# Turnings of the first weight in other PSUM banks, two copies ahead of roundings, and two banks for the last sum, in a fused attention and maxout feed-forward kernel

## The chip, the cores and the metric

The kernel runs on one core of one Trainium2 chip. Its time is the device time of that core in microseconds (us), given as the median of several runs. One execution was also taken with the hardware profiler. All times of instructions below come from that one execution; its span runs from the first to the last instruction that the profiler saw, and its own device time is a little longer than the span.

The engines: TensorE (PE, matrix products; its loads of the stationary operand are listed apart as PEld), VectorE (DVE), ScalarE (ACT), GpSimd (POOL), and SyncE (SP), which here only issues transfers. Each works through its own instructions in program order. PSUM is the memory into which PE writes its products, eight banks of 128 x 512 words of 32 bits; all other data is in SBUF.

## The reference, cut to what matters

```python
# attention: B, H, S, D = 4, 8, 768, 48
f = 1 / (1 + exp(-f_logit))
for t in range(S):
    state = f[:, :, t, :, None] * state + k[:, :, t, :, None] * v[:, :, t, None, :]
    y[:, :, t] = einsum('bhd,bhde->bhe', q[:, :, t], state)
# bridge: heads side by side, x is 3072 x 384
x = y.transpose(0, 2, 1, 3).reshape(3072, 384)
# feed-forward: w1, w2, w3 are 384 x 768, w_out is 768 x 384
h = maximum(maximum(x @ w1, x @ w2), x @ w3)
out = h @ w_out
```

## The kernel before, in words

**Attention.** The sequence is cut into chunks of 64 tokens. A unit is one chunk of two batches with all heads, so 128 rows; there are 24 units, numbered u. For each unit the gates are sigmoids (L308), a scan over them gives the decay from each token to the chunk's end (`scan`, L329), another scan gives the decay from the chunk's start (`before`, L347). k and q are brought to features on partitions by PE transposes (`transposed`, L291), for the early units that matter here, and multiplied with these decays. `keys` transposes the weighted keys (copy ks), `pairs` multiplies keys and queries of a chunk (L392) and masks the result on DVE (L395), `values` multiplies that with v (L407/L411), `sums` makes the chunk's contribution to the state (L436), which for the first two units is copied into the state by ACT (L442) and later added on DVE. `y_by_tokens` copies a finished unit of the first group out of PSUM on ACT, and `x_of_tokens` transposes it on PE and copies it on ACT into `xT`, the transposed x that the feed-forward reads.

**Feed-forward.** Four units make a group of 512 tokens; there are six groups. Groups 1 to 5 use `ffn`, in which products of pairs of blocks are saved by sums taken beforehand (`inputs_by_pairs`, matmuls at L819, and `outputs_by_pairs`, L611, whose helpers `into`, `read` and `add` issue the matmuls, the ACT copies L616 and the DVE additions L619). Group 0 uses `ffn_first`, since the weights are still arriving: `product` (L537) multiplies x with w2 - w1 and w3 - w1, six blocks j of 128 columns, the first three blocks in two half groups of 256 tokens and the last three with all 512. ACT copies the first of each pair to `hm` (L748), DVE takes the maximum with the second and with zero (L750). What is missing, x times w1 w_out, is a linear term: each block of w1 is transposed on PE and written back by ACT (`turn`, L721), and at the end `linear` (L728) multiplies the turned w1 with w_out.

**Weights.** They come as 24 pieces of 384 KB: 18 of w1, w2 and w3, in turn for each block j, and six of w_out. They lie in DRAM as 64-bit numbers, and each piece is rounded to 32 bits: `round_begin` issues two or three ACT activations (L240, L241, L244), `round_end` one or two DVE operations (L251 to L254) and one POOL addition (L258). `round_to(n)` issues `round_end` of the pieces up to n and the `round_begin` of one piece more. `apart` (L699) then subtracts the w1 block from w2 on POOL and from w3 on DVE. `ffn_first` calls `round_to(ROUNDED[n_step])` and `load_weights` after each of its 18 steps, and turns block `TURNED[n_step]` after six of them.

**Order.** The order on each engine is written out by hand: the program is issued as the code stands. `fill(ns)` stands between the attention's steps and draws as many steps of the feed-forward's generator as have that length by an estimate of the matmuls' time. So all that is issued between two steps of `ffn_first` (turning, rounding, transfers) stands in each engine's queue between the attention's instructions around it.

**Banks.** The PSUM pools hand out banks in turn: two named `tr` (attention's transposes of f, k, q, keys and x), one named `a` (pairs, and the first units' sums), one named `y` (values), and two named `p` (the feed-forward). A tile that draws a bank waits until the last reader of the tile that had it has finished. `bank(in_tr)` draws a feed-forward bank from `tr` instead of `p`.

```python
def bank(in_tr=False):
    if in_tr:
        return ps_tr.tile([128, TOK], FP32, name="tr")
    return ps_f.tile([128, TOK], FP32, name="p")
```

q of the first three units is transposed into a `p` bank, that of later units into a `tr` bank, and so is k.

**The start.** Around the change the prologue runs `values(1)`, `y_by_tokens(1)`, `keys(2)`, `round_to(2)`, `sums(1)`, `x_of_tokens(1)`, `scan(3)`, `pairs(2)`, `after(3)` (k), `carry(3)`, `round_to(3)`, `before(3)` (q), `values(2)`, and then the first steps of `ffn_first`.

**The end.** For the last group `outputs_by_pairs` stores its four tiles of 128 tokens as soon as they are ready: each is two transfers of 96 KB (`store`, L556). The second transfer of the last two units is issued on ACT's queue, the others on SP's. The last tiles are made by `into(c, 0, s4, ...)`, an addition of one half on DVE, a store, `into(c, 1, s4, ...)`, the addition of the other half, a store. Both halves lie in one bank, c.

After the last store a flag is read that says whether inputs or weights were outside the range that this fast path takes (L1296); it isn't set here, and the second path is not run.

Of the kernel before, what the change touches and what calls it, by code (L numbers as in the profile page):

```python
# [9 lines left out]
FP32 = mybir.dt.float32  # L10
# [45 lines left out]
def kernel(  # L56
# [12 lines left out]
    nc = tc.nc  # L69
    B, H, S, D = q.shape  # L70
    HP = H // 2
    NU = B // 2 * (S // C)
    UT = 2 * C
    DM = H * D
# [3 lines left out]
    GRP = 4  # L78
    TOK = GRP * UT
# [10 lines left out]
    def fast():  # L90
        ctx = ExitStack()
        with ctx:
# [4 lines left out]
            ps_f = ctx.enter_context(tc.tile_pool(name="ps_f", bufs=2, space=bass.MemoryType.PSUM))  # L97
# [263 lines left out]
            def keys(u):  # L361

                if u < min(BY_ROWS, NU - 2):
                    kh = ready[u]["kh"]
                    tr_s = ps_tr.tile([UT, HP, 128], FP32, name="tr")
                    for hp in range(HP):
                        nc.tensor.transpose(tr_s[:, hp, :], kh[:, hp].rearrange("p a t -> p (a t)"), ident)
                    ks = work.tile([UT, H, DP], FP32, name="ks")
                    nc.scalar.copy(ks.rearrange("s h d -> s (h d)"), tr_s.rearrange("s a d -> s (a d)"))
                    ready[u]["ks"] = ks  # L370
# [114 lines left out]
            def x_of_tokens(u, xT):  # L485
                x = ready.pop(u)["x"]
                tr_x = ps_tr.tile([128, NK, UT], FP32, name="tr")
                for kt in range(NK):
                    nc.tensor.transpose(tr_x[:, kt, :], x[:, kt * 128:(kt + 1) * 128], ident)
                nc.scalar.copy(by_halves(xT)[:, u // 2, :, u % 2 * UT:(u % 2 + 1) * UT], tr_x)  # L490
# [36 lines left out]
# [4 lines that stand above are left out]
# [20 lines left out]
            def store(u, o):  # L551
                c, bp = divmod(u, 2)
                for a in range(2):
                    t0 = (2 * bp + a) * S + c * C
                    last = u >= NU - 2 and a
                    (nc.scalar if last else nc.sync).dma_start(out=out[t0:t0 + C, :], in_=o[a * C:(a + 1) * C, :])  # L556

            def outputs(hm, xT, i):
# [40 lines left out]
            def outputs_by_pairs(g, hm, xT):  # L599
# [9 lines left out]
                def into(b, p, lhs, rhs):  # L609
                    for k in range(HJ):  # L610
                        nc.tensor.matmul(b[:, p * HD:(p + 1) * HD], lhsT=lhs(p)[:, k], rhs=rhs[:, k],  # L611
                                         start=id(b) not in begun, stop=(k == HJ - 1), skip_group_check=True)
                        begun.add(id(b))
# [4 lines left out]
                def add(out, b, n, at=slice(0, 2)):  # L618
                    nc.vector.tensor_tensor(out[:, at], pairs_of(b[:, 0:DM])[:, at], pairs_of(partial[n])[:, at], op=ALU.add)  # L619
# [19 lines left out]
                into(a, 1, s2, w_mix[1])  # L639
                read(a, 1)  # L640
                yield COST
                into(c, 0, s1, w_mix[0])
                yield COST
                into(c, 1, s1, w_mix[0])
                nc.scalar.copy(tops[:, 2], c[:, 0:DM])
                yield COST
                into(a, 0, A(0, 1), w_mix[2])
                yield COST
# [7 lines left out]
                yield COST  # L656
                into(c, 0, X(0), lin[1])
                yield COST
                into(c, 1, X(0), lin[1])
                yield COST  # L660
                into(a, 0, A(1, 1), w_mix[3])
                yield COST
# [14 lines left out]
                    add(o_of(0, 1), c, 1, slice(0, 1))  # L677
                    store(g * GRP, o_four[:, 0])
                yield COST
                into(c, 1, s4, corner(1, 1))  # L680
                if last:
                    add(o_of(0, 1), c, 1, slice(1, 2))
                    store(g * GRP + 2, o_four[:, 2])
                else:
                    add(o_of(0, 1), c, 1)
                    late.extend((g * GRP + i, o_four[:, i]) for i in (1, 3, 0, 2))
# [16 lines left out]
            def round_to(count):  # L703

                for n in range(rounded[0], min(count, len(pieces))):
                    if n + 1 < len(pieces):
                        round_begin(n + 1)
                    round_end(n)
                    if n < 3 * NJ and n % 3 == 1:
                        apart(n, nc.gpsimd)  # L710
                    if n <= 3 * NJ and n and n % 3 == 0:
                        apart(n - 1, nc.vector)
                    rounded[0] = n + 1

            def turn(j):

                p = ps_f.tile([128, TOK], FP32, name="p")
                piece = w_in[0][:, :, j * 128:(j + 1) * 128]
                for a in range(NK):
                    nc.tensor.transpose(p[:, a * 128:(a + 1) * 128], piece[:, a, :], ident)  # L720
                nc.scalar.copy(piece, p[:, 0:DM].rearrange("q (a c) -> q a c", a=NK))  # L721
                yield DM * COLUMN
# [9 lines left out]
                            nc.scalar.copy(w_nat[:, a, :], p[:, 0:DM])  # L732
                        yield 2 * DM * COLUMN

            ROUNDED = (5, 7, 8, 10, 10, 11, 11, 12, 12, 13, 14, 15, 16, 17, 18, 20, 21, 22)
            TURNED = {3: 0, 4: 1, 6: 2, 14: 3, 16: 4, 18: 5}

            def ffn_first(xT):
# [188 lines left out]
            with tc.manual_schedule():  # L927
# [39 lines left out]
                values(1)  # L967
                y_by_tokens(1)
                keys(2)
                round_to(2)  # L970
                sums(1)
                x_of_tokens(1, xT)
                scan(3)
                pairs(2)
                after(3)
# [354 lines left out]
```

## Time and profile before

| | |
|---|---|
| runs (us) | 426.46, 426.51, 427.65 |
| median | 426.51 us |
| the profiled execution | 427.35 us |
| its span | 425.5 us |
| PE busy | 405.3 us (95%), 4650 instructions |
| loads on PE (PEld) | 340.3 us (80%) |
| DVE busy | 265.4 us (62%) |
| POOL busy | 232.8 us (55%) |
| ACT busy | 179.9 us (42%) |
| transfers | 47.20 MB, mean 111 GB/s |
| chain that ended last | PE 86%, DVE 3%, SP's queue 3%, ACT 2%, transfers 2% |

How to read what is quoted later. The page draws the span as 40 slices of 10.6 us; a digit is the busy share of an engine in tenths, and 9 means 90% or more. `PEclk` is the clock granted to PE in tenths of full speed. In the view of waits a line names who waits (engine, tile, line), whom it waited for after `<-` (engine, tile, line), then the total in us, how many waits, and the longest. In the timeline a line gives start and duration in us, engine, line, operation, what it writes and reads with the shapes, how many instructions it puts together, and in brackets the idle time of the engine before it with what ended it. A wait for several semaphores is put down to the one that came last by the profile. In a view of windows the columns are the stretch, its length, the busy time of PE with the instruction count, the mean granted clock, the busy share of the transfer engines, and GB/s.

### The profile page before, as it was taken

To read this page: it belongs to the slowest core of one execution; us is meant where nothing else is said; L and a number is where in the kernel's file an instruction comes from. 1 tells how busy PE (TensorE), PEld (TensorE's weight loads), DVE (VectorE), ACT (ScalarE), POOL (GpSimd) and SP (SyncE) were. 2 spreads that over 40 slices of the span, in tenths; PEclk is the share of its full clock that TensorE was granted. 3 is DMA by queue.
4 is the path that set the end of the run, shared out by engine and by line. 5 is a ranking of instruction groups with operands and counts; after the bars stand their busy time and mean duration, and the time that the engine had idled before them with its cause. 6 is when DMAs were issued, how large, how long until landed. Compare 5 with 4: busy or idle time off the path is not lost.

```text
span 425.5 us, 11548 instructions
## 1 busy us (share of the span) xinstructions
PE 405.3 (95%) x4650; PEld 340.3 (80%) x4650; DVE 265.4 (62%) x517; ACT 179.9 (42%) x413; POOL 232.8 (55%) x260
## 2 busy tenths in 40 slices
PE   5988799899999999999999999999999999999993
PEld 4766665466567888998889988889988899988993
DVE  6986574952687699868789867888774720012300
ACT  2459566732114442425531444442264424576210
POOL 2178354541888676386586357566546960425600
PEclk9989999999999999999999999999999999999998
DMA  8988987771547753276645276634473011542003
GB/s 170 227 262 259 262 241 119 123 173 51 93 95 119 90 128 54 64 96 103 109 122 109 41 116 81 142 82 87 70 151 86 0 53 42 141 129 66 2 1 78
DMA packets 174617, 47.20 MB, mean 111 GB/s; under 512 B 154016, under 2 KB 172256, under 8 KB 174560
## 3 DMA queue, kind: packets, MB, share of 16 engines
q1 hardware_dynamic: 171216, 45.61, 51.6%
q10 hardware_dynamic: 3344, 0.81, 0.9%
q8 instruction: 37, 0.61, 0.6%
q14 instruction: 20, 0.16, 0.1%
HBM read 37.75 MB, written 4.72 MB: 100 GB/s over the span
## 4 chain that ended last, share of the span: by engine, by line
PE 86%; DVE 3%; SPq 3%; ACT 2%; DMA 2%; issue 1%; POOL 1%; DVEq 0%; POOLq 0%
PE p L819 19%; PE tr L819 16%; PE p L611 14%; PE tr L611 12%; PE p L564 6%; PE p L537 5%; PE p L728 3%; PE y L500 3%; PE y L411 3%; PE a L392 2%; DMA raw<-in_moe_w_dram 2%; SPq L174 2%; PE y L436 2%; PE tr L291 1%; SPq L164 1%
## 5 line engine op out<-in xcount | busy, mean ns | idle before, releaser
L819 PE MATMUL tr<-xT,placed 128*128 128x256 f32 x300 | 73.3, 385 | 0.0
L382 DVE STREAM_TRANSPOSE ks<-kh 32x128 f32<-32x128 f32 x224 | 67.7, 302 | 4.6 <-POOL kh L340 1.0
L819 PEld LDWEIGHTS tr<-xT,placed 128*128 128x128 f32 x300 | 55.6, 190 | 9.1 <-ACT hm L827 1.4
L819 PE MATMUL p<-xT,placed 128*128 128x256 f32 x180 | 45.0, 381 | 0.0
L819 PEld LDWEIGHTS p<-xT,placed 128*128 128x128 f32 x180 | 33.8, 190 | 4.7
L537 PE MATMUL p<-xT,w_in 128*128 128x256 f32 (+1 forms) x108 | 34.3, 458 | 2.9 <-DVE hm L750 2.2
L619 DVE TENSOR_TENSOR o<-tr,w_in 128x384 f32<-128x384 f32 (+1 forms) x11 | 5.7, 514 | 49.6 <-PE tr L611 44.3
L329 DVE TENSOR_TENSOR_SCAN r<-gate,from_one 128x520 f32<-128x520 f32 x24 | 31.3, 1306 | 8.3 <-ACT gate L308 5.3
L340 POOL TENSOR_TENSOR kh<-kt,r 128x512 f32<-128x512 f32 x16 | 28.8, 1798 | 10.6 <-DVE kt L296 10.6
L837 POOL TENSOR_TENSOR hm<-hm,rest_bits 128x512 f32<-128x512 f32 x15 | 22.7, 1512 | 19.1 <-ACT hm L827 19.1
L597 POOL TENSOR_TENSOR w_in<-hm 128x256 f32<-128x256 f32 x15 | 10.9, 727 | 40.5 <-DVE hm L870 40.5
L347 DVE TENSOR_TENSOR_SCAN prod<-gate,from_inv 128x520 f32<-128x520 f32 x24 | 32.5, 1355 | 0.0
L506 ACT COPY xT<-y 64x256 f32<-64x256 f32 (+1 forms) x60 | 22.1, 369 | 24.1 <-PE y L500 23.4
L395 DVE TENSOR_TENSOR at<-a,mask 128x512 f32<-128x512 f32 x24 | 16.5, 688 | 24.2 <-PE a L392 23.9
L258 POOL TENSOR_TENSOR w_in<-top_bits,rest_bits 128x384 uint32<-128x384 uint32 x18 | 21.8, 1211 | 15.5 <-DVE top_bits L254 8.8
L819 PE MATMUL p<-w_in,placed 128*128 128x256 f32 x120 | 30.0, 379 | 0.0
L862 DVE TENSOR_TENSOR hm<-tr,hm 128x512 f32<-128x512 f32 x15 | 10.2, 681 | 29.3 <-PE tr L819 19.3
L537 PEld LDWEIGHTS p<-xT,w_in 128*128 128x128 f32 x108 | 19.3, 190 | 10.7 <-issue 6.2
L655 POOL TENSOR_TENSOR o<-top_bits,w_in 128x384 f32<-128x384 f32 x5 | 5.1, 1015 | 41.6 <-ACT w_in L616 41.6
L616 ACT COPY w_in<-p 128x384 f32<-128x384 f32 x15 | 7.2, 479 | 47.1 <-PE p L611 47.1
L280 ACT ACTIVATE raw<-top_bits 128x384 f32<-128x384 f32 x48 | 25.2, 526 | 0.4
L819 PEld LDWEIGHTS p<-w_in,placed 128*128 128x128 f32 x120 | 22.8, 190 | 3.1
(153 smaller groups left out, 890.5 us busy)
## 6 DMA issues: line engine op xcount, KB each, us to landing
raw<-in_moe_w_dram SPq DMA_DIRECT2D x24, 384.0 KB, 4.2
v_ld<-in_v_dram SPq DMA_DIRECT2D x48, 96.0 KB, 3.2
placed<-in_moe_w_dram SPq DMA_DIRECT2D x12, 384.0 KB, 6.6
out_dram<-o SPq DMA_DIRECT2D x46, 96.0 KB, 2.4
placed<-in_moe_w_out_dram SPq DMA_DIRECT2D x6, 384.0 KB, 6.0
raw<-in_moe_w_out_dram SPq DMA_DIRECT2D x6, 384.0 KB, 3.4
f_ld<-in_f_logit_dram SPq DMA_DIRECT2D x32, 64.0 KB, 2.6
k_ld<-in_k_dram SPq DMA_DIRECT2D x32, 64.0 KB, 2.5
```

The source lines that it names most:

```text
L258: nc.gpsimd.tensor_tensor(dst, by(top), by(rest), op=ALU.add)
L280: nc.scalar.activation(over, size, AF.Relu, scale=(-1 / HI_MIN, 1.0)[step - 1], bias=(1.0, -HI_END * (1 - 2.0 ** -24))[step - 1], accum_ou ...
L329: nc.vector.tensor_tensor_scan(r[:, 0:LEN][:, ::-1], flat(gate)[:, ::-1], flat(from_one)[:, ::-1], 1.0, op0=ALU.mult, op1=ALU.max)
L340: (nc.vector if u < BY_ROWS else nc.gpsimd).tensor_tensor(kh.rearrange("p h a t -> p a h t"), kt, by_batch(r[:, 1:LEN + 1].rearrange("p (x ...
L347: nc.vector.tensor_tensor_scan(flat(prod), flat(gate_tiles[u % 2]), flat(from_inv[u % 2]), 1.0, op0=ALU.mult, op1=ALU.max)
L382: nc.vector.transpose(ks[n * 32:(n + 1) * 32, :, par, e0:e0 + 32], kh[p0:p0 + 32, :, a, t0:t0 + 32])
L506: nc.scalar.copy(xT[o, :, t0 + a * C:t0 + (a + 1) * C], y[i, a, 0:HP * C].rearrange("p (h t) -> p h t", h=HP))
L537: nc.tensor.matmul(p if w < TOK else p.rearrange("p (two t) -> p two t", two=2), lhsT=w_in[i][:, kt, j * 128:(j + 1) * 128], rhs=x[:, t.st ...
L564: nc.tensor.matmul(p[:, 0:DM], lhsT=lhsT, rhs=rhs, start=(n == 0), stop=(n == NJ + NK - 1))
L611: nc.tensor.matmul(b[:, p * HD:(p + 1) * HD], lhsT=lhs(p)[:, k], rhs=rhs[:, k], start=id(b) not in begun, stop=(k == HJ - 1), skip_group_c ...
L819: nc.tensor.matmul(b[:, j * HALF:(j + 1) * HALF], lhsT=w[:, (2 * n + j) * 128:(2 * n + j + 1) * 128], rhs=x, start=begin and j == 0, stop= ...
L837: nc.gpsimd.tensor_tensor(out(n, 0), out(n, 0), first, op=ALU.add)
```

## The change

It has four edits.

1. In the prologue, `sums(1)` and `x_of_tokens(1)` move ahead of the rounding of the next weight pieces: `round_to(2)`, `sums(1)`, `x_of_tokens(1)` becomes `sums(1)`, `round_to(1)`, `x_of_tokens(1)`, `round_to(2)`. On ACT the state copy (L442) then stands ahead of two roundings, and the x copy ahead of one.
2. `turn` draws its bank from `tr` for the blocks j = 3, 4 and 5 (`J_HALF` is 3), and from step 13 to the end `ROUNDED` is one piece higher.
3. In `store`, the second transfer of all four units of the last group goes to ACT's queue: four transfers on each queue instead of six and two.
4. In `outputs_by_pairs`, for the last group, the second half of the last sum goes to another bank, b, which is free by then; the copy of the bank's first contents (`tops`) is split into two ACT copies of half the width, one from each bank, and the last addition reads d.

```diff
             def store(u, o):
-                    last = u >= NU - 2 and a
+                    last = u >= NU - GRP and a
...
             def outputs_by_pairs(g, hm, xT):
+                d = b if last else c
                 into(c, 0, s1, w_mix[0])
                 yield COST
-                into(c, 1, s1, w_mix[0])
-                nc.scalar.copy(tops[:, 2], c[:, 0:DM])
+                if last:
+                    begun.discard(id(d))
+                    nc.scalar.copy(pairs_of(tops[:, 2])[:, 0], c[:, 0:HD])
+                into(d, 1, s1, w_mix[0])
+                if last:
+                    nc.scalar.copy(pairs_of(tops[:, 2])[:, 1], d[:, HD:DM])
+                else:
+                    nc.scalar.copy(tops[:, 2], c[:, 0:DM])
...
-                into(c, 1, X(0), lin[1])
+                into(d, 1, X(0), lin[1])
...
-                into(c, 1, s4, corner(1, 1))
+                into(d, 1, s4, corner(1, 1))
                 if last:
-                    add(o_of(0, 1), c, 1, slice(1, 2))
+                    add(o_of(0, 1), d, 1, slice(1, 2))
...
             def turn(j):
-                p = ps_f.tile([128, TOK], FP32, name="p")
+                p = bank(j >= J_HALF)
...
-            ROUNDED = (5, 7, 8, 10, 10, 11, 11, 12, 12, 13, 14, 15, 16, 17, 18, 20, 21, 22)
+            ROUNDED = (5, 7, 8, 10, 10, 11, 11, 12, 12, 13, 14, 15, 16, 18, 19, 21, 22, 23)
             TURNED = {3: 0, 4: 1, 6: 2, 14: 3, 16: 4, 18: 5}
...
                 keys(2)
+                sums(1)
+                round_to(1)
+                x_of_tokens(1, xT)
                 round_to(2)
-                sums(1)
-                x_of_tokens(1, xT)
                 scan(3)
```

## The prediction

> **What bounds the kernel.** The page first: TensorE (PE) is busy 95% of the span and holds 86% of the chain that ended last, so what counts is where PE waits. I read PE's waits next, from 20 to 100 us and from 130 us to the end; then the timeline around each wait; then windows cut where the granted clock steps; then the queues at the end.
>
> ```profile
> PE   5988799899999999999999999999999999999993
> PEclk9989999999999999999999999999999999999998
> ```
> ```profile
> PE p L537 <- DVE hm L750: 2.2, 3, 0.9
> PE a L392 <- ACT st L442: 1.8, 1, 1.8
> ...
> PE p L728 <- POOL state L357: 0.6, 1, 0.6
> ```
> ```profile
> PE tr L611 <- DVE o L619: 0.5, 1, 0.5
> ```
>
> Each line gives total, times and longest. The four parts of the change aim at these four lines: 1.80 us at 21.67, three waits of 0.68, 0.61 and 0.92 at 48.80, 67.17 and 76.77, 0.61 at 84.38, and 0.52 at 418.20. After 130 us PE waits for nothing else: what is won or lost before 100 us reaches the end unchanged.
>
> The first wait, in the timeline (start, duration, engine, line, operation):
>
> ```profile
> 22.50 0.56 ACT L244 ACTIVATE rest_bits<-raw 128x384 uint32<-128x384 uint32 x1 [0.38 <-DMA raw<-in_moe_w_dram]
> ...
> 22.97 0.45 ACT L442 COPY st<-a 128x384 f32<-128x384 f32 x1
> ...
> 23.47 0.75 PE L392 MATMUL a<-qh,kh 48*64 48x64 f32 x32 [1.80 <-ACT st L442]
> 24.16 1.11 PE L291 MATMUL tr<-ident,k_ld 128*128 128x128 f32 x4
> ```
> And PE windows of 3.41 us (length, PE busy, granted clock, DMA share, GB/s):
> ```profile
> 20.54:23.95 3.41, 1.61 (x68) 1.00 0.44 101
> 23.95:27.36 3.41, 3.41 (x48) 0.50 0.99 302
> ...
> 41.02:44.43 3.41, 2.07 (x40) 1.00 1.08 376
> ```
> A window with 1.61 us of PE work (47%) is followed by one at half clock; one with 2.07 us (61%) is not. So a wait costs its length and, where it empties a window, a slow window as well.
>
> **Part 1, state and x copies ahead.** ScalarE's (ACT's) state copy now follows the ks copy (20.96, ends 21.54); its matmuls L436 end at 21.19. It starts near 21.57 instead of 22.97, and the pairs L392 at 22.07, 1.40 earlier. The x copy stands behind one rounding, ends near 22.9, and then lets the q transposes go. What is late next: the values L407 need the masked product L395 on VectorE (DVE), 24.35 to 25.0, behind the scan L329 of 22.96, which stands behind roundings of landed weights and does not move. So L407 starts at 25.05, not 26.05: -1.0. At full clock it takes 1.17 (row of 18.83), not 1.75: -0.6. The first product L537 of the feed-forward follows at 26.2, not 27.73 (GpSimd's difference L699 it needs is done at 26.08): -1.5. The second product at 30.45 gains only 0.35: GpSimd (POOL) works without a gap from 23.19, its sum L258 ends at 29.46 and DVE's L699 follows. But the hm copy on ACT (29.33) moves 1.5, ACT is gapless behind it, and the o copy of 35.93 on the chain moves with it. Then landing limits: weight piece 9 is issued at 34.09 and lands 3.7 later, 37.8, and its rounding ran at 38.77 (-1.0); piece 10, 34.8 plus 4.4, 39.2 against 40.24 (-1.0). Chain alone: -1.9. I take **-1.4**, between. The other end is 0: in an execution whose clock is not halved at 23.95, q would end at 25.05 in the old order too and L407 would start no later than now.
>
> **Part 2, turnings in the transpose banks, roundings one step earlier.** The waits of 67.17 and 76.77 come from the product drawing the bank of the last product, because the turning has taken the other one; these go (-0.61, -0.92). The wait at 84.38 is put down to POOL's state, but the instruction waits for DVE and POOL, and DVE's hm, 83.54 to 84.23, frees its bank: it goes as well (-0.61). The one at 48.80 stays, since turning 2 keeps its bank. A new wait comes. There are two transpose banks; after the turning of j = 4, k draws one and q draws the turning's own. So q must wait for ACT's copy of the turning, last in this queue:
>
> ```profile
> 73.96 0.60 ACT L308 ACTIVATE gate<-tr 128x512 f32<-128x512 f32 x1
> 74.45 0.55 ACT L240 ACTIVATE top_bits<-placed 128x384 f32<-128x384 f32 x1
> ...
> 76.90 0.55 ACT L244 ACTIVATE rest_bits<-placed 128x384 uint32<-128x384 uint32 x1
> 77.35 0.46 ACT L721 COPY w_in<-p 128x384 f32<-128x384 f32 x1
> ```
>
> Gate, six rounding activations, copy: done at 77.81, or 77.2 with the 0.61 won before. Moving the roundings does not shorten it: two of them still stand ahead of this copy. PE ends k near 74.65 and stands 2.5 us. Behind q in PE's order wait product, values and sums, and none can pass. The product starts at 77.65 instead of 76.77: +0.88; with -0.61 at 84.38, **+0.25** in all. Ends: -2.1 (no new wait) and +0.9 (the wait at 84.38 stays).
>
> The rounding moved up costs nothing while its covers hold: three activations (1.5 us) fall before ACT's idle 67.05 to 70.02, DVE's two operations (0.55 each) into its 5.02 us idle before 73.27. Without those covers they would delay the masked product by up to 1.1. The w1 copy of turning 3, 0.8 later, is wanted only by the f transposes at 72.5.
>
> Clock: 2.5 us of standing in windows of 3.41. Halving needs between 1.34 us (39% idle, not enough) and 1.80 us of idle in one window. Over all positions of the window that happens in (3.41 + 2.5 - 2T)/3.41, 68% (T = 1.80) to 95% (T = 1.34). Price: dense PE work at half clock for at most 3.41 us, 1.7; part of the slow window may fall into the standing itself. I take **+1.3**, ends 0 and 1.7.
>
> The Trainium skill, page "TensorE: Matmul & The Clock Gate", section "HAM oscillation — how this bites in real kernels", lets the clock fall only after gaps of more than about 3.4 us. This trace differs: it fell after 1.80 us. By the page the 2.5 us would not halve the clock and the sum would be 424.7; the measurement decides.
>
> **Parts 3 and 4, the end.**
>
> ```profile
> 417.29 4.66 SPq L556 DMA_DIRECT2D out_dram<-o  x6
> ...
> 418.20 1.24 PE L611 MATMUL tr<-w_out,w_in 128*128 128x192 f32 x6 [0.52 <-DVE o L619]
> 419.48 0.36 DVE L619 TENSOR_TENSOR o<-tr,w_in 128x192 f32<-128x192 f32 x1 [1.33 <-PE tr L611]
> ```
>
> With its own bank the second half follows the first: 416.70 + 0.97 = 417.67 instead of 418.20, and the pipe is not refilled; DVE's last addition moves from 419.48 to about 418.75 and ends at 419.1: -0.74. The one copy L645 (0.48) becomes two of half the width; ACT stands idle 3.42 us before its next copy at 410.89, which hides them, and PE asks for neither bank before 410.7. SP now issues its six stores between 417.29 and 420.4, where the last starts 0.56 after its data is ready and takes 1.51 to issue; the last completion SP waits for comes at 423.7. With four per queue the last two go at 419.13. They land 2.4 (the first stores' landing) to 3.3 us (the last one's) later, 421.5 to 422.4; eight stores of 96 KB at the 215 to 240 GB/s of that stretch need 3.3 to 3.7 us from 418.2, so 421.5 at the least. Gain 1.3 to 2.2; if the transfers fill the time whatever the queues, 0.74. I take **-1.5**. From 423.7 to 425.5 nothing changes.
>
> The skill's page "DMA: Bandwidth & Descriptors", section "Issuing engines are not separate DMA queues", says that a second issuing engine saves only issue time, usually small. By that the split would add 0.56 to the 0.74, and the sum would be 0.2 higher.
>
> **The sum.** The profiled execution took 427.35 (span 425.5 and 1.85 around it): 427.35 - 1.4 + 0.25 + 1.3 - 1.5 = **426.0**. It stands 0.84 above the median of 426.51 (runs 426.46, 426.51, 427.65); I read the difference as mostly the slow window at 23.95, which not every execution needs to have.
>
> **Rivals.**
> - Forecast, the standing at q happens and halves the clock: 426.0. For it: bank order and ACT's queue are fixed by the program, and 47% was enough to halve. Chance 0.50.
> - The standing happens, the clock stays: 424.7. For it: 61% was not enough to halve, and the window's position is free. Against: 2.5 us is longer than the 1.80 that did it. 0.28.
> - The slow window only moves, from 24 us to 77 us. Most executions then have no early gain (start at the lower runs, 426.5), pay 0.25 and the full 1.7, and get only the 0.74 at the end: 427.7, slower than before. It decides as soon as the window around q has under about half PE work and the one around 22 us had more. For it: the runs shown spread over 1.2 us, the size of such a window. Against: ACT's o copy is on the chain. 0.15.
> - The stores do not do what they should, because the last landing is set by the transfers: 426.0 + 0.76 = 426.8. 0.07.
>
> **The numbers.** About 0.3% (1.28 us: 425.23 to 427.79) is what a measurement of this kernel can tell from no change. Faster: most of the second case (0.24) and a fifth of the first (0.10), 0.34. Slower: about half of the third, 0.08. The rest, 0.58, is within. The range runs from below the second case (its early gain at 1.9) to the third less 0.3: 424.0 to 427.4.
>
> **What would show it.** L392 starts near 22.1 and its wait is under 0.5; no slow window at 24; L407 at 25. Waits of L537 for hm at 67 and 77 gone; instead the q transposes wait some 2.5 us for ACT's w_in copy, followed by about 3.4 us at clock 0.5. The L611 wait for DVE o is gone; both queues issue their last store within 0.1 us after DVE's last addition, and the last completion comes 1.3 to 2.2 us earlier. I would be wrong if q does not wait, if half clock spreads over a second window, or if product L537 at 27.7 has not moved.

## The result, and the profile after

Over 20 runs each, the changed kernel takes **427.65 us** against **427.37 us**: ratio 1.0002, 95% interval 0.9988 to 1.0016. That is no change that can be measured. The forecast was 426.0 with a range up to 427.4, so the time lies just outside it, on the side of the third rival. The kernel before has come out higher as well: three runs had given 426.51. One of the changed kernel's 20 runs took 595.28 us at a granted clock of 0.66; such slow runs are left out of every ratio here.

The profiled execution of the changed kernel has a span of 426.5 us against 425.5, +1.0 where the sum on record has -1.35. The same instruction in both timelines shows where it came from (start, us; the last two rows are ends):

| instruction | before | after | difference |
|---|---|---|---|
| pairs L392 of unit 2 | 23.47 | 21.89 | -1.58 |
| values L407 of unit 2 | 26.05 | 24.96 | -1.09 |
| first product L537 | 27.73 | 26.05 | -1.68 |
| second product | 30.45 | 30.35 | -0.10 |
| fourth product | 37.15 | 36.78 | -0.37 |
| check of the state L473 | 43.33 | 43.47 | +0.14 |
| product near 48.8 | 48.80 | 48.95 | +0.15 |
| q transposes L291 | 75.25 | 77.15 | +1.90 |
| state product L500, next unit | 87.56 | 89.19 | +1.63 |
| last sum, first half L611 | 416.54 | 418.18 | +1.64 |
| last addition L619 | 419.84 | 420.69 | +0.85 |
| span | 425.5 | 426.5 | +1.0 |

The page shows the one slow window, now in the eighth slice, 75 to 85 us (before, a digit 8 in the third):

```profile
PEclk9999999899999999999999999999999999999999
```

So part 1 ends at +0.15 (on record -1.4), part 2 with the clock costs 1.49 (on record 1.55), and parts 3 and 4 give 0.65 (on record 1.5). These are differences between two single executions; that of before had a half clock at 24 us, that of the changed kernel has none there.

PE's waits in the changed kernel, from 15 to 135 us (who <- whom: us in total, times, longest):

```profile
PE tr L291 <- ACT w_in L728: 2.4, 1, 2.4
PE p L537 <- DVE w_in L706: 2.2, 2, 1.7
PE p L473 <- DVE st L444: 1.5, 1, 1.5
PE y L407 <- DVE at L395: 1.3, 1, 1.3
```

The wait for ACT's state copy is down to 0.3. In its place PE waits for DVE, on three lines (L473's wait was 1.0 before), and at q for ACT's w_in copy, 2.4 us as foreseen. In the early timeline (start, duration, engine, line, operation, idle time before and what ended it):

```profile
21.89 0.69 PE L392 MATMUL a<-qh,kh 48*64 48x64 f32 x32 [0.26 <-ACT st L442]
24.96 1.17 PE L407 MATMUL y<-v_ld,at 64*64 64x48 f32 x32 [1.35 <-DVE at L395]
...
30.35 1.56 PE L537 MATMUL p<-xT,w_in 128*128 128x256 f32 x6 [1.68 <-DVE w_in L706]
```

Of the 1.6 us won at L392 and at the first product all but 0.10 is given back in the 1.68 before the second. Around q, the row of its transposes and windows of 3.41 us laid on the steps of the clock (stretch, length, PE busy, granted clock, share of the transfer engines, GB/s):

```profile
77.15 1.04 PE L291 MATMUL tr<-ident,q_ld 128*128 128x128 f32 x4 [2.44 <-ACT w_in L728]
```
```profile
73.90:77.31 3.41, 0.97 (x9) 0.99 0.79 102
77.31:80.73 3.42, 3.42 (x8) 0.51 0.59 69
```

The standing (PE without work until q can start) leaves PE 0.97 us of work in a window, and the next window is at half clock. And the end (the queues' lines give first issue and total stretch):

```profile
418.92 3.01 SPq L556 DMA_DIRECT2D out_dram<-o  x4
418.93 3.30 ACTq L556 DMA_DIRECT2D out_dram<-o  x4
...
420.33 0.36 DVE L619 TENSOR_TENSOR o<-tr,w_in 128x192 f32<-128x192 f32 x1 [0.55 <-PE tr L611]
```

The two halves follow each other without the 0.52 us wait, but the last stores go out at 421.39 (SP) and 421.61 (ACT), 0.7 and 0.9 after the last addition.

### The profile page after: what moved, and what is told of

The parts are those of the page before. It is cut to its first block, busy times and chain, and to the rows that moved or that the text cites. A ratio compares the mean times of both kernels' runs of the same rounds, so it can differ in the third digit from the quotient of the medians.

```text
span 426.5 us, 11551 instructions
## 1 busy us (share of the span) xinstructions
PE 404.1 (95%) x4650; PEld 339.3 (80%) x4650; DVE 266.2 (62%) x517; ACT 179.9 (42%) x414; POOL 233.1 (55%) x260
## 4 chain that ended last, share of the span: by engine, by line
PE 87%; SPq 5%; DMA 2%; ACT 2%; POOL 1%; DVE 1%; issue 1%; ACTq 0%
PE p L826 19%; PE tr L826 16%; PE p L611 14%; PE tr L611 11%; PE p L537 6%; PE p L564 6%; PE y L411 3%; PE y L500 3%; PE p L735 3%; SPq L164 2%; PE a L392 2%; PE y L436 2%; SPq L174 2%; DMA placed<-in_moe_w_dram 2%; PE tr L291 1%; SPq L218 1%
## 5 line engine op out<-in xcount | busy, mean ns | idle before, releaser
L537 PE MATMUL p<-xT,w_in 128*128 128x256 f32 (+1 forms) x108 | 35.6, 471 | 3.5 <-DVE w_in L706 2.2
L619 DVE TENSOR_TENSOR o<-tr,w_in 128x384 f32<-128x384 f32 (+1 forms) x11 | 5.7, 515 | 48.8 <-PE tr L611 43.5
L506 ACT COPY xT<-y 64x256 f32<-64x256 f32 (+1 forms) x60 | 22.1, 368 | 24.1 <-PE y L500 23.4
L258 POOL TENSOR_TENSOR w_in<-top_bits,rest_bits 128x384 uint32<-128x384 uint32 x18 | 21.8, 1217 | 15.4 <-DVE top_bits L254 7.7
L537 PEld LDWEIGHTS p<-xT,w_in 128*128 128x128 f32 x108 | 19.9, 196 | 11.9 <-issue 5.6
L280 ACT ACTIVATE raw<-top_bits 128x384 f32<-128x384 f32 x48 | 25.2, 526 | 0.4
```

The lines of the kernel that those rows point to most:

```text
L258: nc.gpsimd.tensor_tensor(dst, by(top), by(rest), op=ALU.add)
L280: nc.scalar.activation(over, size, AF.Relu, scale=(-1 / HI_MIN, 1.0)[step - 1], bias=(1.0, -HI_END * (1 - 2.0 ** -24))[step - 1], accum_ou ...
L506: nc.scalar.copy(xT[o, :, t0 + a * C:t0 + (a + 1) * C], y[i, a, 0:HP * C].rearrange("p (h t) -> p h t", h=HP))
L537: nc.tensor.matmul(p if w < TOK else p.rearrange("p (two t) -> p two t", two=2), lhsT=w_in[i][:, kt, j * 128:(j + 1) * 128], rhs=x[:, t.st ...
```

## The experiments

The experiments set the theory on record (ACT's copies are what PE waits for early; the standing at q halves the clock; four stores a queue land earlier) against a rival for each part that the traces suggested. Every kernel was compared with the kernel before on the same chip; the medians of before were 427.79, 427.42, 427.33 and 427.65 in the four groups.

| kernel | us | ratio to before (95%) | half clock in its profile, us |
|---|---|---|---|
| p1_only | 427.43 | 0.9991 (0.9977 to 1.0005) | 30.4 |
| p2_only | 428.24 | 1.0012 (0.9997 to 1.0027) | 76.7 |
| end_only | 427.0 | 0.9982 (0.9965 to 0.9999) | none |
| after_turn4_in_p | 424.92 | 0.9931 (0.9910 to 0.9952) | 24.9, 45.4 |
| light_weights | 425.4 | 0.9965 (0.9941 to 0.9989) | none |
| light_weights_p1 | 424.54 | 0.9934 (0.9916 to 0.9953) | 44.4 |
| after_filler | 427.21 | 0.9997 (0.9983 to 1.0010) | 30.2, 43.9 |
| turn4_in_p_early | 429.11 | 1.0043 (1.0024 to 1.0063) | 25.6 |
| after_filler_5 | 426.28 | 0.9980 (0.9966 to 0.9993) | none |
| turn4_in_a | 423.07 | 0.9898 (0.9876 to 0.9919) | 30.6 |
| stores_only | 426.84 | 0.9989 (0.9975 to 1.0004) | none |
| turn4_in_p_old_roundings | 425.63 | 0.9957 (0.9939 to 0.9974) | none |
| light_dve | 425.43 | 0.9948 (0.9933 to 0.9963) | none |
| light_pool | 424.23 | 0.9929 (0.9912 to 0.9947) | 23.4 |
| turn4_in_a_no_part1 | 423.85 | 0.9923 (0.9909 to 0.9936) | none |
| turn4_in_a_old_stores | 423.93 | 0.9923 (0.9906 to 0.9940) | 45.4 |

The last column gives where each half-clock stretch of the profiled execution begins. Each is one window of 3.41 us, except that of turn4_in_p_early, which is two. Those after the last matmul are left out.

**Each part alone.** p1_only is part 1 in the kernel before:

```diff
                 keys(2)
-                round_to(2)
                 sums(1)
+                round_to(1)
                 x_of_tokens(1, xT)
+                round_to(2)
```

> Part 1 alone in the kernel before. The theory on record: -1.4 us, whichever execution, because the copies were the last thing PE waited for. New theory (the stream of weights is the bound from 24 to 50 us: both profiles issue pieces 9 to 11 at 34.1 to 34.2 and the first use after that moved only from 40.73 to 40.44, then to +0.15): between -0.4 and +0.2 us. In its profile L392 starts near 22 and L407 near 25 by both; by the new theory the check matmul L473 near 43.3 and the product near 48.8 stay within 0.3 us of the kernel before, counted from the first weight's landing.

-0.4 us (-1.0 to +0.2). L392 starts at 21.78 and L407 at 24.59, but the product near 48.8 is at 48.84: nothing is left of it there. The new theory's number holds, at its edge; its cause, the landings of the weights, does not (below). The profiles with a full clock up to 50 us say the same: this product starts at 48.24 to 49.17 in the old order (p2_only, end_only, stores_only, turn4_in_a_no_part1) and at 48.23 to 48.95 in the new (the changed kernel, after_filler_5, turn4_in_p_old_roundings).

p2_only has the new banks for the turnings and the new `ROUNDED`:

> Part 2 alone (turnings of j = 3, 4, 5 in the transpose banks, later roundings one earlier) in the kernel before. Theory: PE stands 2.4 us at the q transposes near 77 for ACT's w_in copy, the clock is halved for 3.41 us after it, +0.25 for the waits and +1.7 for the clock where it is halved: +1.0 to +2.0 us. Rival (the standing only takes the place of other waits and the clock has no part): 0 to +0.3 us, with no window at clock 0.5 after 77 us.

+0.5 us (-0.1 to +1.2) in time, so under what was expected of it; in the profile the 2.4 us wait at L291 and the half clock at 76.7 are there. From the product that starts at 57.47 before (56.91 here) to the third group of L500 it is 46.78 us, the same as in the changed kernel and 1.49 more than before (45.29). This stretch hardly varies: in all eight profiles with the old part 2 it is 45.29 or 45.30. That the time shows less than 1.49 would fit executions in which the standing falls across two windows and halves nothing, but no run here shows how many do.

end_only has parts 3 and 4:

> Parts 3 and 4 alone (two banks for the last sum, four stores on each queue). The theory on record: -1.5 us, 0.74 from the bank and the rest from stores that land earlier. New theory, from the profile of the changed kernel: the bank gives 0.7 to 0.8 and the stores nothing, since with two queues issuing at once each issue takes about twice as long (1.1 to 1.2 us against 0.59) and the last store still goes out 0.7 to 0.9 us after the last addition: -0.6 to -0.8 us.

-0.8 us (-1.5 to 0.0). From the copy of the last group's first finished tiles (L677) to the end of the span it is 8.16 us, against 8.80 before (L670) and 8.14 in the changed kernel; how much this varies is told below.

**Where part 2 pays, and the clock.** after_turn4_in_p is the changed kernel with one turning back:

```diff
-                p = bank(j >= J_HALF)
+                p = bank(j in (3, 5))
```

> The changed kernel, with turning j = 4 alone put back into the feed-forward's own banks (3 and 5 stay in the transpose banks). Theory of the standing at q: the 2.4 us wait of L291 goes, the wait of the product L537 for hm near 77 (0.9) comes back, the halved clock after 77 goes; against the kernel before the waits at 67 and 84 stay won (0.6 each) and the end 0.64: -1.5 to -2.0 us against before, and -1.5 to -2.5 against the changed kernel. Rival (weight roundings set the pace there, so that what is won at q is lost at the next weight): within 0.5 us of the changed kernel.

424.92, -2.9 us against before (-3.8 to -2.1): more than forecast, although its profile has two windows at half clock. The product of 57.47 is 0.80 late there (the half clock at 45.4), and the third group of L500 is 0.90 early, so part 2 in this form is worth 1.70: the two waits of 0.61 and some 0.2 us of refilling at each. One bank decides over part 2's sign.

after_filler keeps PE busy during the standing; after_filler_5 does so with the right number of matmuls:

```diff
                         after(n)
+                        if n == GRP + 2:
+                            spare = ps_a.tile([UT, 2, 512], FP32, name="a")
+                            for _ in range(8):
+                                nc.tensor.matmul(spare[:, 0, 0:256], lhsT=ident, rhs=flat(from_one)[:, 0:256], start=True, stop=True)
                         before(n)
```

> The changed kernel, with eight matmuls of 128x256 whose result nobody reads, in the bank of the pairs, put between the k and q transposes where PE stands for 2.4 us near 75. Theory of the clock: the standing keeps its length or grows by at most 0.2 us, but no window near 77 is at half clock any more, so that -1.3 to -1.7 us against the changed kernel; about 426.0. Rival (the half clock does not come from the standing, or comes anyway): the same time as the changed kernel within 0.3 us.

> The changed kernel with five unread matmuls between the k and q transposes near 75, where the run with eight filled 3.62 us and so held q up by about 1 us; five are 2.26 us by that row, a little less than the 2.44 us that PE stands. Theory of the clock: q starts where it does in the changed kernel, within 0.2 us, at full clock, and from the start of one L500 (near 71.4) to that of the next (near 89.2) it is 16.1 us in the profile, 17.8 in the changed kernel; the time is 1.2 to 1.7 us below the changed kernel's, about 426.2. Rival: 17.8 us as before, same time.

The first missed its number: eight such matmuls ran as sixteen passes in 3.62 us and held q up until 78.20, and two early windows were at half clock; the one near 77 was gone there too. The second is the clean test. Its q transposes and the window there:

```profile
76.49 0.66 PE L291 MATMUL tr<-ident,q_ld 128*128 128x128 f32 x4 [0.34 <-ACT w_in L728]
```
```profile
73.45:76.86 3.41, 3.07 (x18) 1.00 0.78 96
76.86:80.28 3.42, 3.42 (x51) 1.00 0.63 89
```

The standing is as long, but it is filled; the clock stays, the stretch from the first group of L500 to the second takes 16.21 us against 17.82 in the changed kernel, and the time is -0.9 us against before (-1.5 to -0.3), where the changed kernel has +0.1; by the ratios that is 0.9 won, a little under what was expected. The half clock comes from PE's lack of work in the standing and costs 1.6 to 1.7 us (1.61 here, with q 0.07 later than in the changed kernel, counted from the first group of L500).

turn4_in_a puts turning 4 where no one waits for its copy:

```diff
-                p = bank(j >= J_HALF)
+                p = ps_a.tile([128, 2, 512], FP32, name="a")[:, 0] if j == 4 else bank(j in (3, 5))
```

> The changed kernel with turning j = 4 in the bank of the pairs, which has been free since the masked product of 74.1 and is wanted again at 87; 3 and 5 stay in the transpose banks. Theory of the banks: neither the q transposes nor the product near 76.7 wait, so that the 0.92 us wait and some 0.2 us of refilling go as well: 0.9 to 1.2 us below the run with turning 4 in its old bank, 423.5 to 424.0 us. Rival (what PE waits for there is the weights' rounding, whatever the bank): the same as that run within 0.3 us.

423.07 us, **-4.4 us against before (-5.3 to -3.5), the fastest version here** and a little under the 423.5 that was the least expected. Its timeline at the place of the standing:

```profile
73.92 0.60 PE L291 MATMUL tr<-ident,q_ld 128*128 128x128 f32 x4
74.35 2.74 PE L537 MATMUL p<-xT,w_in 128*128 128x512 f32 x6
```

Neither waits. By the profiles 2.85 of the 4.4 us is part 2 in this form (42.44 from the product of 57.47 to the third group of L500, against 45.29). From the first group of L500 to the second it is 13.48 us, 1.16 less than with turning 4 in its old bank (14.64): the bank, not the rounding, was what PE waited for.

turn4_in_p_old_roundings takes the other half of part 2 out (and has `j in (3, 5)`):

```diff
-            ROUNDED = (5, 7, 8, 10, 10, 11, 11, 12, 12, 13, 14, 15, 16, 18, 19, 21, 22, 23)
+            ROUNDED = (5, 7, 8, 10, 10, 11, 11, 12, 12, 13, 14, 15, 16, 17, 18, 20, 21, 22)
```

> The changed kernel with turning j = 4 back in its old bank and the roundings as they were before. Theory on record: the rounding moved up costs nothing and gains nothing, so that the time is within 0.3 us of the run with turning 4 in its old bank (424.92). Rival (the earlier rounding is what took the wait at 84 away): 0.5 to 0.8 us more, with PE's wait of L735 for POOL back.

425.63, 0.7 more in the medians and 1.1 by the ratios (the two ran on different chips), and the same stretch is 15.29 against 14.64, 0.65 more. The rival is right: with the bank free, the first `linear` waits for the last rounded pieces.

```profile
85.35 0.91 PE L735 MATMUL p<-w_out,w_in 128*128 128x384 f32 x2 [0.38 <-POOL w_out L258]
```

**Where part 1 went.** light_weights leaves the early subtractions out:

```diff
-                    if n < 3 * NJ and n % 3 == 1:
+                    if 9 <= n < 3 * NJ and n % 3 == 1:
                         apart(n, nc.gpsimd)
-                    if n <= 3 * NJ and n and n % 3 == 0:
+                    if 9 < n <= 3 * NJ and n % 3 == 0:
                         apart(n - 1, nc.vector)
```

> The kernel before without the subtraction of w1 from the first six of the w2 and w3 blocks (three of 1.0 to 1.25 us on POOL and three of 0.55 to 1.34 us on DVE, between 25 and 43 us); the output is not the reference's. Theory now: DVE and POOL, with the roundings and these subtractions, end level with the copies of part 1, so taking work from them alone moves the product near 48.8 by 0.5 to 1.5 us. The theory on record (the copies on ACT are what PE waits for): that product stays within 0.3 us.

The product near 48.8 comes at 46.57, 2.2 us earlier, more than either theory had, with ACT's order untouched (L392 at 23.33) and the ninth weight piece landing when it did before (37.57 and 37.77). So neither ACT's copies alone nor the landings were what this product waited for.

> The same with part 1; the same subtractions are left out. Theory now: with DVE and POOL out of the way part 1 is worth something, 0.5 to 1.4 us against the run without part 1, in the product near 48.8 and in the time. Rival (the landings of the weights are the bound, near 29.6 and 38.8 us): below 0.3 us.

The fourth product comes at 35.14 against 35.48, so part 1 is worth 0.34 there; then ACT waits for the ninth weight piece, which landed at 38.15 against 37.57, and the state check comes at 41.66 against 41.09. The rival holds at that place: with DVE and POOL lighter, the landing is next. In time part 1 gives 0.9 us here in the medians, which intervals of 0.8 and 1.0 to either side do not tell from nothing. In both runs the check comes 3.5 us after that landing. In the changed kernel the piece landed at 38.84 and the check came 4.6 us after it, so there the landing was not what held it; but by the same 3.5 us it would have let the check come no earlier than 42.4, 1.0 before the 43.33 of the kernel before. (The product near 48.8, at 48.21, also carries a half clock from 44.4.)

light_dve and light_pool make only the second or only the first of the two edits.

> The kernel before without DVE's three subtractions of w1 from early w3 blocks (0.55, 0.54 and 1.34 us, before 43 us); the output is not the reference's. If DVE holds the stretch: the product near 48.8 comes 1.3 to 2.2 us earlier, as without the subtractions of both engines. If POOL holds it: under 0.5 us.

> The kernel before without POOL's three subtractions of w1 from early w2 blocks (1.0 to 1.2 us each, before 40 us); the output is not the reference's. If POOL holds the stretch: the product near 48.8 comes 1.3 to 2.2 us earlier. If DVE holds it: under 0.5 us.

```profile
46.19 1.56 PE L537 MATMUL p<-xT,w_in 128*128 128x256 f32 x6 [0.68 <-DVE hm L750]
```
```profile
47.49 1.56 PE L537 MATMUL p<-xT,w_in 128*128 128x256 f32 x6 [0.68 <-DVE hm L750]
```

The product near 48.8 in light_dve (first) and light_pool (second): 2.6 and 1.3 us earlier. (light_pool's profile has a half clock at 23.4, light_dve's none.) Neither "under 0.5" came true: both engines are on the chain, in turn. The times say the same (-2.2 and -3.0 us, each interval 0.7 wide to either side), and cannot rank them.

turn4_in_p_early tried the landings:

```diff
                 load_weights(3)
+                load_weights(6)
                 load_v(2)
                 load_v(3)
-                load_weights(6)
```

> The changed kernel with turning j = 4 back in its old bank, as in the run that took 424.92 us, and weight pieces 3 to 8 issued ahead of the v tiles of units 2 and 3, so that they land about 1 us earlier. Landing theory: the product near 48.8 and the time move by -0.7 to -1.0 us. Theory of DVE and POOL: DVE is without a gap from 22.4 to 31.6 us whatever lands, so within 0.3 us of that run.

429.11, 4 us worse than after_turn4_in_p: the edit made a new wait, for v of unit 2, and so it does not tell the two theories apart.

```profile
PE y L407 <- DMA v_ld<-in_v_dram: 4.7, 1, 4.7
```

turn4_in_a_no_part1 takes part 1 out of the fastest kernel:

> The kernel with turning 4 in the bank of the pairs, without part 1. Theory now (in an execution with a full clock at 24 us the values L407 start near 24.9 in either order, since they wait for DVE's masked product; DVE's chain sets the product near 48.8 also where the clock was halved): within 0.3 us of the run with part 1, 423.07. The theory on record: 1.4 us more.

423.85, 0.8 more in the medians, not the 0.3 expected; the two ratios differ by 0.0025 with about that much uncertainty, so the time does not decide. L407 starts at 25.21 against 24.89, although it is the old order and L392 still waits:

```profile
23.57 0.69 PE L392 MATMUL a<-qh,kh 48*64 48x64 f32 x32 [1.74 <-ACT st L442]
...
25.21 1.17 PE L407 MATMUL y<-v_ld,at 64*64 64x48 f32 x32
```

In the two profiles the state check L473 differs by 0.86 (42.84 and 43.70), and nearly all of it is one operation of DVE just before it, first with part 1, then without:

```profile
41.68 0.55 DVE L706 TENSOR_TENSOR w_in<-w_in,w_in 128x384 f32<-128x384 f32 x1
```
```profile
41.76 1.33 DVE L706 TENSOR_TENSOR w_in<-w_in,w_in 128x384 f32<-128x384 f32 x1 [0.90 <-POOL w_in L258]
```

In the second, POOL's next sum L258 had begun just before. The changed kernel itself has the slow form there (1.34 at 41.52). Whether part 1 makes the quick order likelier stays open.

**The end, part by part.**

```diff
-                    last = u >= NU - 2 and a
+                    last = u >= NU - GRP and a
```

> Part 3 alone, four stores on each queue, in the kernel before. The theory on record: -0.76 us. Theory now: nothing, within 0.2 us, the time from the last addition to the end of the span staying at 5.6 to 5.9 us, since issues on two queues at once take 1.1 to 1.2 us each where one alone takes 0.59.

> The kernel with turning 4 in the bank of the pairs, with the stores six on SP and two on ACT as before, the last sum in two banks. Theory now: the bank's 0.79 us is kept but the stores, which start from the same time, end no earlier than without it, as SP's last issue stands behind five others; the end comes 0.1 to 0.6 us later than in the run with four stores on each queue. Rival (the stores do nothing once the bank is there): within 0.1 us in the profile from the copy of the first finished half to the end of the span, 8.1 us.

"Nothing" for stores_only was a miss in the profile: 8.36 us from the copy to the span's end instead of 8.80, and 5.27 us behind the last addition where 5.6 to 5.9 was expected. The time, 426.84 or -0.5 us (-1.1 to +0.2), does not decide. With the bank there it is 7.98 us with four a queue and 8.26 with six and two, in the kernels with turning 4 in a. But such single figures (0.44 for the stores alone, 0.54 for the bank with the old stores) lie within what this stretch varies by: with the old end it is 8.51 to 9.48 us over seven profiles (mean 8.80), with both parts 7.85 to 8.57 over nine (mean 8.17). Both together are worth 0.63 in the mean. What does not vary is the bank's share, the time from the copy to the end of the last addition: 3.10 us in the eight profiles without it (3.09 in one), 2.31 in the ten with it. From there to the span's end it is 5.41 to 6.38 with the old end (mean 5.70) and 5.54 to 6.26 with both parts (mean 5.86), so beside the bank the stores win nothing that can be seen. Issues of the stores, min/median/max in ns, in the changed kernel:

```profile
L556 SPq DMA_DIRECT2D out_dram<-o x4: 473/545/1207, 418.9 to 421.4; - x4
L556 ACTq DMA_DIRECT2D out_dram<-o x4: 579/738/1121, 418.9 to 421.6; - x4
```

and in stores_only:

```profile
L556 SPq DMA_DIRECT2D out_dram<-o x4: 466/510/591, 416.8 to 419.3; - x4
L556 ACTq DMA_DIRECT2D out_dram<-o x4: 499/596/769, 416.8 to 419.3; - x4
```

When the last addition comes 0.79 earlier, the stores ahead of it are still being issued, and an issue takes up to 1.2 us instead of 0.6 to 0.8; the last two wait behind them. In the nine profiles with both parts they go out 0.33 to 0.98 us (SP) and 0.57 to 1.22 us (ACT) after the last addition; in stores_only, 0.02 and 0.03 after it.

## Why the prediction was wrong

**Part 1 is the step that failed** (on record -1.4, measured +0.15 in the profile, -0.4 with -1.0 to +0.2 in time). Its first links were right to 0.3 us: L392 at 21.89 (22.07 on record), L407 at 24.96 (25.05), the first product at 26.05 (26.2), the second hardly moved (-0.10, on record -0.35). The link that failed is "the o copy of 35.93 on the chain moves with it". The copy did move, by 1.39, but what it released had another wait right behind it:

```profile
34.54 0.46 ACT L481 COPY o<-y 128x384 f32<-128x384 f32 x1
...
36.78 1.53 PE L537 MATMUL p<-xT,w_in 128*128 128x256 f32 x6 [0.52 <-DVE w_in L706]
...
40.14 2.30 POOL L258 TENSOR_TENSOR w_in<-top_bits,rest_bits 128x384 uint32<-128x384 uint32 x2
...
41.52 1.34 DVE L706 TENSOR_TENSOR w_in<-w_in,w_in 128x384 f32<-128x384 f32 x1 [0.89 <-POOL w_in L258]
```

In this timeline of the changed kernel the product waits for DVE's subtraction, that one for POOL's sums, and DVE's next again for POOL's, up to the state check at 43.47. The working saw this alternation ahead of the second product and did not follow it on. The same subtraction ahead of the fourth product, in the changed kernel (first) and before:

```profile
35.30 1.34 DVE L706 TENSOR_TENSOR w_in<-w_in,w_in 128x384 f32<-128x384 f32 x1 [0.89 <-POOL w_in L258]
```
```profile
35.40 0.54 DVE L699 TENSOR_TENSOR w_in<-w_in,w_in 128x384 f32<-128x384 f32 x1
...
35.62 1.18 POOL L258 TENSOR_TENSOR w_in<-top_bits,rest_bits 128x384 uint32<-128x384 uint32 x1 [0.56 <-ACT top_bits L241]
```

Before, POOL's next sum began only after DVE's subtraction had started. In the changed kernel POOL's sums follow each other from 33.95 to 36.22, the subtraction starts inside the second and takes 0.80 longer (the last section has this for all profiles), and POOL's sum after it starts at 37.85 instead of 37.36. So the 0.52 us that PE waits for this subtraction at the fourth product come from a collision of DVE with POOL. The landing limit was mis-sized as well: piece 9, put at 37.8, landed at 38.84, 4.6 us after its issue and not 3.7.

The end given as 0, for an execution with a full clock at 24 us, was the common case: of eight profiled kernels with the old order two had the half clock near 24, and in the other six L407 started at 24.3 to 25.2 without part 1. Even where it was halved, as in the profile of before, the loss was covered by the product near 48.8: 48.80 there, 48.85 in end_only with the old order and a full clock. The subtraction near 35 us (38.7 in turn4_in_p_early) goes with it: of the 15 profiles that have it, it takes 0.54 or 0.55 in the four with a half clock that begins between 23.4 and 25.6 us, and 1.34 or 1.35 in the other eleven. So in these profiles a late start escapes the collision and wins 0.8 us back.

**The q stall was right.** PE stood 2.44 us for 2.5, and the wait at 84 is gone. The product came 0.66 later where +0.88 was forecast, if the 0.40 of slowed q transposes and the 0.15 from part 1 are taken off the 1.21. Without the clock part 2 gives -0.1 to -0.2 for +0.25 (45.16 in after_filler_5 against 45.29); the wait of 0.61 at 67, when it went, brought 0.78, so some 0.2 of refilling goes with a wait. That the wait at 84 goes by the bank alone was half right: it goes to 0.38 by the bank, and to nothing by the rounding moved up, which on record "costs nothing" and indeed costs nothing, but gains 0.65.

**The clock was right in kind and low in size**: 1.6 to 1.7, the upper end named, for the 1.3 that was taken. The gap of about 3.4 us that the Trainium skill names (page "TensorE: Matmul & The Clock Gate", section "HAM oscillation — how this bites in real kernels") did not decide here; 2.44 was enough, and after_filler_5 shows it.

**The end was mis-sized**: 0.79 from the bank for 0.74, but some 0.13 was lost again behind the last addition (5.83 us to the span's end against 5.70) where 0.76 was to be won. The step that failed is "with four per queue the last two go at 419.13", right after the last addition: they went 0.7 and 0.9 after it, since the issues ahead of them were not done. From issue to landing the stores then took 2.3 to 3.2 us, as allowed for. The bound from the transfers was read from peaks: 215 to 240 GB/s were taken, and the single microseconds from 418 to 423 in the kernel before moved 110 to 238. The Trainium skill's rule that a second issuing engine saves only issue time (page "DMA: Bandwidth & Descriptors", section "Issuing engines are not separate DMA queues") was the better guide, though even the 0.56 that the working drew from it was not won beside the bank.

The three parts add up: part 1 is 1.55 over its term in the profile, the end 0.85, part 2 with the clock 0.06 under, together the 2.35 between the -1.35 on record and the +1.0 measured.

**The third rival's number, 427.7, came true, by most of its mechanism**: no early gain, the full clock price, and just the bank's share at the end. Part of that is luck: it was added to 426.5, and the kernel before has come out at 427.37; as a change the rival says +1.2, and measured is +0.1 (-0.5 to +0.7). Its reason for the missing gain, a full clock at 24 us, is only half of it, since the gain is missing where the clock was halved too. It was given 0.15, as ACT's o copy was taken to be on the chain; and the early gain was read from one execution with a slow window that most do not have. That no measurable change was the likeliest outcome (0.58) was right, but not for the reasons given.

What stays open is the sum in time: the three parts alone add up to -0.7 us, the whole shows +0.1 by its ratio, each with 0.6 to 0.7 of uncertainty, so the two do not contradict each other; the profiles give +1.0 for the whole. Executions of one kernel differ in their mean granted clock, from 0.983 to 0.999 in the changed kernel; the lowest of the 20, 425.14 with a mean clock of 0.999, is near the 424.7 on record for a standing without the half clock.

## What to carry to other kernels

When a wait is removed, walk on from the released instruction on every engine that feeds it until one chain is clear of the others by more than the gain; where two engines hand work to each other in turn, what a third does earlier can be lost in them. A bank that is free is not enough: ask which copy must be done before the next user draws it, and what is queued ahead of that copy. A standing of PE has two prices, its length and what it does to the clock; filling it with matmuls that nobody reads leaves only the first to pay.

## What the runs showed of the hardware

**The clock goes by a window's share of work, not by a gap.** Half-clock stretches last 3.41 us (6.83, two windows, in turn4_in_p_early), and the windows can be laid on their steps. Over the 18 profiles, between 12 and 85 us, all five windows at full clock with PE busy for less than 49% were followed by half clock; of 13 with 49 to 58.5%, eight; of those above, none. Two of after_turn4_in_p (first) and one of turn4_in_a:

```profile
42.00:45.41 3.41, 1.76 (x42) 0.99 1.08 378
45.41:48.82 3.41, 3.28 (x11) 0.51 0.91 253
```
```profile
40.82:44.23 3.41, 2.18 (x40) 1.00 1.09 377
```

52% was followed by half clock, 64% was not. Three places of this kernel (near 21, 28 and 41 us) lie close to the limit in these profiles. Executions may therefore differ by a window or two there, which would hide small shifts in the time; that is argued, since only one execution of each kernel was profiled.

**DVE and POOL get in each other's way.** DVE's subtraction of 128x384 took 0.55 or 1.34 us. Over the 18 profiles 67 took 0.54 to 0.56, and no POOL operation was running when they began; in the 32 that took 1.33 to 1.35 POOL's sum had begun 0.07 to 0.08 before, and they ended 0.41 to 0.42 after it. In the changed kernel POOL's second L258 ends at 42.44, and L706 at 42.86, 0.42 later. The Trainium skill, page "SBUF — State Buffer", section "SBUF: two separate sides", says that the port pair that DVE and GpSimd share is an exclusive lock, for a DVE operation with two inputs in SBUF as for this one, held for the whole instruction, and that the loser blocks fully; the runs agree. So a chain that alternates between the two engines pays for both, and 0.8 us can hang on which of them starts first.
